# Attention on transposed scores, two heads side by side on the halves of TensorE, in a fused attention and feed-forward kernel

## The chip, the cores and the metric

The kernel runs on one core of a Trainium2 chip. The metric is device time in microseconds, from repeated executions; the trace of one execution gives the span from first to last instruction (1 to 2 us shorter). Engines: PE is TensorE's matmuls, PEld its weight loads, DVE is VectorE, ACT ScalarE, POOL GpSimd, SP the queue that issues most transfers.

## The reference

Attention within hash buckets (a query sees only the keys with the same 6 sign bits), then a feed-forward block with the gate h * erf(softplus(h)).

```python
# q, k, v: (4, 8, 768, 64) fp32; proj: (64, 6)
q_bucket = sum(((q @ proj) > 0) * 2**arange(6));  k_bucket = ...   # per token
scores = where(q_bucket[..., :, None] == k_bucket[..., None, :], q @ k.T / 8, -1e9)
attn = exp(scores - scores.max(-1)); attn = attn / (attn.sum(-1) + 1e-9)
x = (attn @ v) laid out as (3072, 512)
h = x @ w_in                       # (512, 2048)
out = (h * erf(max(h, 0) + log1p(exp(-abs(h))))) @ w_out    # (2048, 512)
```

## The kernel before

One head at a time, 128 queries at a time. The bucket is matched inside the score product: 64 rows of q, then 64 rows of a one-hot bucket, against k and -2^100 where the bucket differs. So each score matmul contracts 128 rows. The softmax runs along the free axis, which needs a maximum, and the result must be transposed before it can weigh v.

```python
def attend(i, c):                       # head i, chunk c of 128 queries
    for half in range(2):
        nc.tensor.matmul(out=sc[:, half, 0:HS], lhsT=d["qa"][:, c*P:(c+1)*P],
                         rhs=d["ka"][:, half*HS:(half+1)*HS], start=True, stop=True)
    nc.vector.reduce_max(out=m, in_=sc[:, :, 0:HS], axis=AX.XY)
    ...                                  # nm = -scale * m
    nc.scalar.activation(out=e, in_=sc, func=AF.Exp, bias=nm, scale=scale, accum_out=z)
    ...                                  # r = 1 / (z + 1e-9);  e = e * r
def turn(i, c, e):                       # six 128x128 transposes, two evictions on ACT
    ...
def weigh(i, half):
    for kc in range(NC):                 # output in 64 partitions: 64 columns of the array
        nc.tensor.matmul(out=av[rows, :], lhsT=d["vt"][:, kc, :], rhs=d["eT"][:, kc, :], ...)
    nc.vector.tensor_copy(out=xT[b][rows, h // 2, ...], in_=av[rows, :])
```

Meanwhile the fp64 weights are loaded and rounded to fp32. The feed-forward stage follows: per period 64 matmuls of the hidden layer and 16 of the output layer, with ACT and DVE computing the gate beside them. The change hardly touches it.

## Time and profile before

| | us |
|---|---|
| time, median of 4 | 1456.19 (1453.61 to 1458.48) |
| attention with its start | 785 |
| feed-forward | 671 |
| TensorE busy, of the span | 97% |

A line of a group reads: source line, engine, operation, output<-inputs, shapes, count | busy time, mean ns of one | idle time of the engine just before, and what ended it. Each fp32 matmul shows as two records. A matmul's mean ns is its latency; what it costs is the spacing of records in the chain of waits, whose lines read start, length, what, count. The prediction below shows the lines of before.

### The profile page before, as it was taken

How to read it: one execution, taken by the hardware profiler on the slowest of the kernel's cores; microseconds unless marked ns; L12 is line 12 of the kernel's file. 1: busy time of each engine (PE TensorE's matmuls, PEld its weight loads, DVE VectorE, ACT ScalarE, POOL GpSimd, SP SyncE). 2: the span in 40 equal slices, each digit the busy share in tenths (PEclk: the TensorE clock that was granted, in tenths of full speed). 3: DMA queues.
4: the chain of work that ended last, by engine and by line, in shares of the span. 5: the costliest groups of instructions: out<-in, count | busy, mean ns of one | idle time of the engine just before them, and what ended most of it. 6: DMA issues, size and time to landing. Idle time of an engine off the chain costs nothing.

```text
span 1455.9 us, 14558 instructions
## 1 busy us (share of the span) xinstructions
PE 1418.3 (97%) x5248; PEld 803.2 (55%) x5248; DVE 1058.9 (73%) x1868; ACT 799.2 (55%) x1201; POOL 144.5 (10%) x102
## 2 busy tenths in 40 slices
PE   7999999999999999999999999999999999999998
PEld 3444444444444444544446866666666666666653
DVE  6888888879887666667662896686686686686684
ACT  2344444444444444445443886676676676676683
POOL 3432143324320000000000000000000000000000
PEclk9999999999999999999999999999999999999999
DMA  5221222212211011111000000000000000000000
GB/s 161 73 70 61 77 75 59 75 60 82 71 53 36 31 44 28 38 28 39 6 1 1 0 0 15 15 1 15 15 1 15 15 0 15 15 0 15 15 1 29
DMA packets 40703, 49.17 MB, mean 34 GB/s; under 512 B 27308, under 2 KB 27320, under 8 KB 40632
## 3 DMA queue, kind: packets, MB, share of 16 engines
q1 hardware_dynamic: 35856, 31.47, 7.2%
q0 software_dynamic: 4608, 16.78, 3.6%
q8 instruction: 41, 0.67, 0.2%
q14 instruction: 30, 0.25, 0.1%
q10 hardware_dynamic: 168, 0.01, 0.0%
HBM read 41.96 MB, written 6.29 MB: 33 GB/s over the span
## 4 chain that ended last, share of the span: by engine, by line
PE 79%; DVE 14%; ACT 2%; issue 2%; POOL 1%; DMA 1%; SPq 0%; ACTq 0%; POOLq 0%; DVEq 0%
PE o_ps L477 21%; PE h_ps L399 21%; PE av L334 14%; PE sc L276 12%; PE tr_ps L319 7%; DVE m L284 3%; PE bits_ps L227 2%; DVE e L304 2%; ACT e L291 1%; DVE qa L254 1%; PE bucket_ps L246 1%; DVE top L197 1%; DVE keep L170 1%; DVE ka L262 1%; DMA qa<-in_qkT_dram 1%
## 5 line engine op out<-in xcount | busy, mean ns | idle before, releaser
L326 ACT COPY eT<-tr_ps 128x384 f32<-128x384 f32 x384 | 171.2, 481 | 321.0 <-PE tr_ps L319 319.7
L477 PE MATMUL o_ps<-w_out_sb,h 128*128 128x512 f32 x768 | 338.5, 595 | 3.6 <-DVE h L466 3.6
L399 PE MATMUL h_ps<-xT,w_in_sb 128*128 128x256 f32 x1536 | 338.5, 379 | 0.0
L399 PEld LDWEIGHTS h_ps<-xT,w_in_sb 128*128 128x128 f32 x1536 | 291.8, 190 | 57.7 <-issue 13.0
L276 PE MATMUL sc<-ka,qa 128*128 128x384 f32 x768 | 299.3, 498 | 11.8 <-ACT e L291 11.1
L334 PE MATMUL av<-eT,vt 128*64 128x384 f32 x768 | 262.8, 492 | 0.0
L477 PEld LDWEIGHTS o_ps<-w_out_sb,h 128*128 128x128 f32 x768 | 146.3, 191 | 171.1 <-issue 162.6
L284 DVE TENSOR_REDUCE m<-sc 128x1 f32<-128x768 f32 x192 | 183.3, 954 | 64.1 <-PE sc L276 61.0
L291 ACT ACTIVATE e<-sc,nm 128x768 f32<-128x768 f32 x192 | 174.1, 907 | 89.9 <-DVE nm L286 87.4
L319 PEld LDWEIGHTS tr_ps<-ident,e 128*128 128x128 f32 x1152 | 127.0, 141 | 120.9 <-issue 49.5
L334 PEld LDWEIGHTS av<-eT,vt 128*64 128x64 f32 x768 | 100.4, 137 | 154.7 <-issue 146.6
L319 PE MATMUL tr_ps<-ident,e 128*128 128x128 f32 x1152 | 177.8, 282 | 7.8 <-DVE e L304 3.5
L276 PEld LDWEIGHTS sc<-ka,qa 128*128 128x128 f32 x768 | 126.4, 192 | 69.6 <-ACT e L291 25.9
L412 ACT COPY h<-h_ps 128x1024 f32<-128x1024 f32 x48 | 48.5, 1011 | 171.3 <-PE h_ps L399 171.3
L458 DVE SCALAR_TENSOR_TENSOR s<-q,s 128x1024 f32<-128x1024 f32 x96 | 111.1, 1220 | 23.0 <-ACT q L457 23.0
L304 DVE TENSOR_SCALAR e<-e,r 128x768 f32<-128x768 f32 x192 | 124.3, 647 | 2.8
L341 DVE COPY xT<-av 64x384 f32<-64x384 f32 x64 | 35.3, 551 | 94.4 <-PE av L334 94.3
L457 ACT ACTIVATE q<-z,cq 128x1024 f32<-128x1024 f32 x96 | 102.1, 1134 | 0.0
L486 DVE COPY ob<-o_ps 128x512 f32<-128x512 f32 x24 | 16.5, 690 | 109.3 <-PE o_ps L477 109.3
L173 POOL TENSOR_SCALAR keep<-keep 128x512 int32<-128x512 int32 x32 | 73.2, 2287 | 92.8 <-DVE nm L286 56.8
L466 DVE TENSOR_TENSOR h<-h,s 128x1024 f32<-128x1024 f32 x48 | 56.6, 1221 | 16.7 <-ACT s L465 16.7
L413 DVE TENSOR_SCALAR e<-h 128x1024 int32<-128x1024 int32 x48 | 33.1, 690 | 45.0 <-ACT h L412 45.0
(43 smaller groups left out, 1100.5 us busy)
## 6 DMA issues: line engine op xcount, KB each, us to landing
qa<-in_qkT_dram SPq DMA_DIRECT2D x32, 384.0 KB, 3.4
raw<-in_w_in_dram POOLq DMA_DIRECT2D x16, 512.0 KB, 4.2
raw<-in_w_out_dram POOLq DMA_DIRECT2D x16, 512.0 KB, 3.8
ka<-in_qkT_dram SPq DMA_DIRECT2D x32, 192.0 KB, 3.7
vt<-in_v_dram SPq DMA_DIRECT2D x32, 192.0 KB, 2.6
out_dram<-ob SPq DMA_DIRECT2D x24, 256.0 KB, 2.0
powers_f<-in_powers_dram ACTq DMA_DIRECT2D x1, 6.0 KB
proj_sb<-in_proj_dram SPq DMA_DIRECT2D x1, 6.0 KB, 1.7
```

Of the source, the lines that this page charges most:

```text
L173: nc.gpsimd.tensor_scalar(out=keep, in0=keep, scalar1=float((1023 - 126) << 20), scalar2=-1.0, op0=ALU.is_ge, op1=ALU.mult,)
L276: nc.tensor.matmul(out=sc[:, half, 0:HS], lhsT=d["qa"][:, c * P : (c + 1) * P], rhs=d["ka"][:, half * HS : (half + 1) * HS], start=True, s ...
L284: nc.vector.reduce_max(out=m, in_=sc[:, :, 0:HS], axis=AX.XY)
L291: nc.scalar.activation(out=e[:, :].rearrange("p (h k) -> p h k", h=2), in_=sc[:, :, 0:HS], func=AF.Exp, bias=nm[:, 0:1], scale=scale, accu ...
L304: nc.vector.tensor_scalar(out=e, in0=e, scalar1=r[:, 0:1], scalar2=None, op0=ALU.mult)
L319: nc.tensor.transpose(out=ps[:, j * P : (j + 1) * P], in_=e[:, kc * P : (kc + 1) * P], identity=ident,)
L326: nc.scalar.copy(out=dst, in_=src)
L334: nc.tensor.matmul(out=av[rows, :], lhsT=d["vt"][:, kc, :], rhs=d["eT"][:, kc, :], start=(kc == 0), stop=(kc == NC - 1),)
L399: nc.tensor.matmul(out=ps[:, f, :], lhsT=w_in_sb[:, kc, (g * G + f) * P : (g * G + f + 1) * P], rhs=xT[b][:, kc, t0 : t0 + T], start=(kc = ...
L457: nc.scalar.activation(out=q, in_=z, func=AF.Square, bias=cq[:, j : j + 1])
L458: nc.vector.scalar_tensor_tensor(out=s, in0=q, scalar=r, in1=s, op0=ALU.add, op1=ALU.mult)
L477: nc.tensor.matmul(out=ps, lhsT=st[t * NG + f // G]["h"][:, f % G, tt * P : (tt + 1) * P], rhs=w_out_sb[:, f, :], start=(f == 0), stop=(f ...
```

## The change

Scores are computed transposed (keys on partitions), so exp's output can weigh v without any transpose. Heads go in pairs: the scores of head A contract rows 0-63 of the array and those of head B rows 64-127; the weighted sums of A leave through columns 0-63 and those of B through columns 64-127. The bucket mask becomes a bf16 matmul of sign bits that is accumulated ahead of the fp32 scores. No maximum is subtracted: exp is safe while a bound on |scores|, checked on the chip during the feed-forward stage, is at most 40. If not, a branch at the end repeats everything by a general path (not taken with these inputs). Sums over keys, now along partitions, are added up on VectorE and finished by a matmul with ones; the divisors go through DRAM to be inverted compactly and broadcast. A query with no matching key gets the mean of v: half of the weighted sums have a 385th column, of ones, for it, and its scaled result is `ev` below.

```diff
-        def attend(i, c):      # score, max, exp with bias and sum, scale
-        def turn(i, c, e):     # transposes and evictions
+            def scores(n):
+                d["st"] = [big("st") for _ in range(GC)]
+                for part, src in enumerate(("b", "")):        # bf16 bits, then fp32
+                    for c in range(GC):
+                        for ab in range(2):
+                            rows = slice(ab * D, ab * D + D)
+                            nc.tensor.matmul(out=d["st"][c][:, ab, 0:HS],
+                                lhsT=d["k" + src][rows, keys], rhs=d["q" + src][rows, cols], ...)
+            def sum_keys(n):   # d["sum"] += e, on VectorE, 128x768 a time
+            def weigh(n):
+                for c in range(GC):
+                    for ab in range(2):
+                        rows = slice(ab * D, ab * D + D)
+                        nc.tensor.matmul(out=d["av"][rows, 0:w],
+                            lhsT=d["v"][:, g * GC + c, rows], rhs=e[:, ab, 0:w], ...)
+            def divisor(n):    # ones x sum, both heads
 ...
+            for n in range(NS + 4):          # 16 pairs x 4 steps
+                scores(n); taking = bits(i + 1, r)
+                sum_keys(n - 1); weigh(n - 1)
+                exponentials(n); taking()
+                if (n - 1) % 2 == 1: divisor(n - 1); leave(n - 1)
+                if r == 0 and i >= 1: spread(i - 1)      # z to DRAM and back, compact
+                if r == 2 and i >= 1: invert(i - 1)      # 1/z to DRAM, broadcast back as r
+                if r == 3 and i >= 1: normalise(i - 1)   # x = (x + ev) * r, on VectorE
 ...
+            def extremes(m):   # feed-forward: reload q and k, absolute maxima on VectorE
+    def judge():               # bound of all heads: a load, a product, flag
+    again = nc.values_load(flag[0:1, 0:1], min_val=0, max_val=1)
+    with tc.If(again > 0):
+        general()
+        feed_forward(None)
```

## The prediction

> **What bounds the kernel now.** I read the page first (who is busy), then the groups by form (what the busy engine does), then the two stages as windows, then the chain of waits inside one head.
>
> From the page: the totals, the utilisation row of TensorE, and the chain that ended last.
>
> ```profile
> PE 1418.3 (97%) x5248; PEld 803.2 (55%) x5248; DVE 1058.9 (73%) x1868; ACT 799.2 (55%) x1201; POOL 144.5 (10%) x102
> ...
> PE   7999999999999999999999999999999999999998
> ...
> PE 79%; DVE 14%; ACT 2%; issue 2%; POOL 1%; DMA 1%; SPq 0%; ACTq 0%; POOLq 0%; DVEq 0%
> ```
>
> TensorE is busy 97% from the second slice on, and is 79% of the chain. The kernel is bound by TensorE in both stages, so a change is worth what it takes out of TensorE's stream, as long as no other engine comes up behind it.
>
> The two stages, from the windows view (attention, then feed-forward; the first scores start at 14.15 us and the last weighted sum ends at 784.8 us):
>
> ```profile
> 14.00:785.00 771.00, 749.36 (x2936) 364.27 (x2936) 585.33 (x1399) 350.98 (x769) 139.96 (x92) 1.00 0.17 50
> 785.00:1456.00 671.00, 663.31 (x2304) 437.83 (x2303) 468.32 (x457) 448.19 (x432) 0.00 (x0) 1.00 0.03 10
> ```
>
> Columns are window, length, then busy time and count of PE, PEld, DVE, ACT, POOL. Attention takes 785 us with its start and feed-forward 671 us; TensorE fills both (97% and 99%).
>
> The groups of the attention stage on TensorE, and the work on ACT and DVE that the change touches:
>
> ```profile
> L276 PE MATMUL sc<-ka,qa 128*128 128x384 f32 x768 | 299.3, 498 | 11.8 <-ACT e L291 11.1
> L334 PE MATMUL av<-eT,vt 128*64 128x384 f32 x768 | 262.8, 492 | 0.0
> L284 DVE TENSOR_REDUCE m<-sc 128x1 f32<-128x768 f32 x192 | 183.3, 954 | 64.1 <-PE sc L276 61.0
> L291 ACT ACTIVATE e<-sc,nm 128x768 f32<-128x768 f32 x192 | 174.1, 907 | 89.9 <-DVE nm L286 87.4
> L326 ACT COPY eT<-tr_ps 128x384 f32<-128x384 f32 x384 | 171.2, 481 | 321.0 <-PE tr_ps L319 319.7
> L304 DVE TENSOR_SCALAR e<-e,r 128x768 f32<-128x768 f32 x192 | 124.3, 647 | 2.8
> L319 PE MATMUL tr_ps<-ident,e 128*128 128x128 f32 x1152 | 177.8, 282 | 7.8 <-DVE e L304 3.5
> ```
>
> Scores 299, weighted sums 263, transposes 178; with bits 51.5 and buckets 34.5 (two smaller rows of the same view) that is the 750 us above, give or take overlap. The 492 ns mean of one record is its latency; the cost is the spacing. The chain of waits gives it (start, length, what, records):
>
> ```profile
> 704.21 4.01 PE av L334 x12
> 708.22 0.80 PE tr_ps L319 x6
> 709.03 1.29 PE sc L276 x4
> 710.32 0.66 PE tr_ps L319 x6
> ```
>
> Scores: 1.29/4 = **0.322 us a record** of 384 columns. Each fp32 matmul is two records (192 score chunks x 2 halves = 384 matmuls, 768 records), so 0.644 us. Twelve av records should take 12 x 0.322 = 3.86 and take 4.01; six transposes right after av take 0.80, elsewhere 0.66. So going into and out of the 64-column form costs about **0.15 us** each time.
>
> **What the Trainium skill says.**
> 1. "TensorE: Matmul & The Clock Gate", section "Part 3: Packing small matmuls — row/col tiling": matmuls with other row or column groups run concurrently, starts some 4 ns apart, and still issue in order; 4 row tiles gave 3.07x, 3 column tiles 2.38x. The trace before has no two groups side by side, so it neither agrees nor disagrees.
> 2. "TensorEngine Tiling (Array Packing)", section "Key Properties": a change of the tiling mode drains the engine. The trace agrees, with the 0.15 us above.
> 3. "FP8 and Floating Point Precision", section "TensorE Precision Notes": true fp32 is four passes. [...]So a bf16 matmul of 384 columns is half a record, an estimate of 0.16 us.
> 4. "VectorE: DVE Perf Modes", section on the TRN2 errata: an fp32 tensor_tensor takes (N+151)/0.96 ns. For 1024 that is 1224; the trace has 1221 to 1225. For 768 it gives 957 ns.
>
> **The change, part by part.** A step of the new loop is 384 queries x 3 key chunks x 2 heads; 16 pairs x 4 = 64 steps.
>
> *Removed from TensorE:* all transposes (178 us) and the bucket matmuls (34 us). *Moved onto half arrays:* scores now contract 64 rows and the two heads of a pair lie in rows 0-63 and 64-127; the weighted sums of the two heads lie in columns 0-63 and 64-127. The mask becomes an extra bf16 matmul per score tile. *Added:* divisor matmuls. Bits stay: 64 fp32 matmuls.
>
> The instruction order is head A, head B, A, B, with both records of A ahead of B's. If issue is in order, A's second record waits for A's first, then B's first starts beside A's second: overlap two deep, one record late. N records in one mode then take (N/2+1) x 0.322. TensorE per step:
> - hash part: 6 bf16 matmuls, 3 x 0.16 = 0.5.
> - fp32 scores: 12 records, 7 x 0.322 = 2.25.
> - bits of the next pair: 2 x 0.322 = 0.64 (absent in the last 4 steps).
> - weighted sum: 12 records, 2.25; in every other step with 4 divisor records, 9 x 0.322 = 2.90; mean 2.58.
> - three mode switches, 3 x 0.15 = 0.45.
>
> Sum 6.42; x 64 = 411; less 3 for the missing bits, plus 3 for the last weighted sum: **411 us**.
>
> Beside it, ACT: a 384-column eviction takes 481 ns and a 1024-column one 1011, so 0.83 ns a column plus 163; 768 columns without the accumulator read about 800. 192 exps = 154, 32 signs of q = 15, 64 evictions = 31, 64 weight operations of 512 at 0.59 = 38: 238 us, 58% of 411. All eT copies (171) go. DVE: 160 sums of 768 at 0.957 = 153; weight rounding 568+697+695+412+677 ns = 3.05 a piece, x 32 = 98; bits of k 32 x 0.62 = 20; normalising 16 x 0.96 = 15: 286 us, 70%. Both fit under TensorE. The score buffers: step n+1 needs the three PSUM tiles that ACT empties in step n; ACT ends them about 1.5 us after the last score, while TensorE has bits and weighted sum (over 3 us) to do. No new wait if the overlap is as assumed. The divisors' round trips through DRAM have two to three steps, 13 us or more, of slack.
>
> *Start:* first scores at 14 us before. Now four bit matmuls pass one PSUM bank one by one: 17 us. *Feed-forward:* 48 halves of 6.9 us each for both products are unchanged: 671. New there: 64 loads and 64 absolute maxima of 384 columns (0.55 us by the 954 ns row), 35 us of DVE, in a stage where DVE is 70% busy; two buffers, so DVE also waits for loads. Off the path; I allow 6 us. *End:* flag read and branch on each engine, 4 us. The general path is not run.
>
> Sum: 17 + 411 + 671 + 6 + 4 = 1109. I add 2% of the attention (8) for waits that a tight loop always has, and 1.3 as runs are longer than the span: about **1118 us**, 0.77 of before.
>
> **The rivals.**
> - *The halves do not overlap* (fp32 in two records, in-order issue). Per step: 0.96 + 3.86 + 0.64 + 14 x 0.322 + 0.45 = 10.4, x 64 = 667. Time 17 + 667 + 681 + 9 = about 1370. For it: nothing in the trace shows overlap, and the skill's runs are not said to be fp32. Against: weight loads are already hidden behind the matmul before (137 ns in 322).
> - *Only one kind overlaps.* Rows not: 2.07 more a step, 132 us, about 1250. Columns not (two fp32 streams through all 128 rows): 1.93 more, 124 us, about 1240.
> - *DVE or ACT becomes the bound.* DVE at 286 of 411 would have to be slowed 40%, or waits on the round trips must block it. It would give 1150 to 1200. ACT would need more still.
> - *The check in feed-forward delays gates*: DVE from 70% to over 80% with load waits; up to 30 us, 1150.
> - *Better than assumed*: no lag of one record, 0.322 less twice a step: 1080.
>
> **Range and chances.** Full overlap 65%, one kind only 20%, none 13%, something unforeseen 2%. Even without overlap the removed transposes and buckets leave it 6% faster. So 1118, range 1070 to 1245 (it takes in the one-kind rivals, and leaves out no overlap). Faster 0.95, within 2% 0.03, slower 0.02.
>
> **What the changed profile would show.** Right: attention's last matmul near 430 us, steps of 6.4 to 6.6 us with TensorE still 95% busy, score tiles of two heads finishing within one record of each other, twelve weighted-sum records in about 2.3 us; ACT near 240 and DVE near 290 in attention; feed-forward within 10 us of 671; ACT waiting for TensorE and not the reverse. Wrong: scores or weighted sums 0.322 apart a record (no overlap); TensorE idle ahead of scores because of exponentials, or ahead of divisors because of the DVE sums; switches much above 0.15 us; feed-forward halves above 6.9 us.

## The result, and the profile after

| | before | after |
|---|---|---|
| time, median | 1456.19 us | 1128.34 us (1125.14 to 1134.24, 4 runs) |
| ratio | | 0.7754, 95% interval 0.7719 to 0.7788 |
| first scores start | 14 us | 18 us |
| attention after that | 771 us | 423 us |
| feed-forward to the last instruction | 671 us | 685 us |

A ratio is the mean time of one kernel's fast runs over that of the other's of the same rounds, so not quite the ratio of the medians quoted. The predicted 1118 us with 1070 to 1245 held. From the page of after, the same rows as shown of before, with the granted clock by slice added:

```profile
PE 1057.3 (94%) x4482; PEld 608.6 (54%) x4482; DVE 809.8 (72%) x962; ACT 678.0 (60%) x785; POOL 77.9 (7%) x68
...
PE   5999898999989987989999999999999998999987
...
PEclk9999999999999998999999999999999998999999
...
PE 75%; DVE 12%; DMA 8%; issue 2%; ACT 1%; SPq 1%; DVEq 0%
```

TensorE is still the bound, but in the attention slices (the first sixteen) it is no longer full, and the chain now runs for 8% through transfers, where before it was 1%. The groups by form say who is waiting:

```profile
L308 PE MATMUL st<-q,k 64*128 64x384 f32 x768 | 140.8, 501 | 0.0
...
L344 PE MATMUL av<-e,v 128*64 128x385 f32 x384 | 69.2, 495 | 0.0
L344 PE MATMUL av<-e,v 128*64 128x384 f32 x384 | 68.8, 494 | 0.0
...
L308 PE MATMUL st<-qb,kb 64*128 64x384 bf16 x384 | 45.7, 347 | 0.0
...
L356 PE MATMUL z_ps<-sum,ones 128*64 128x384 f32 x128 | 29.9, 545 | 36.8 <-DVE sum L332 36.8
...
L417 DVE SCALAR_TENSOR_TENSOR xT<-xT,ev,r 128x768 f32<-128x768 f32 x16 | 16.3, 1019 | 41.4 <-DMA r<-rd 41.4
```

Scores and weighted sums have as many fp32 records as before (768 each), but 141 and 138 us of busy time in place of 299 and 263. The transposes are gone. The last two lines are a pair: VectorE stands 41.4 us before normalising, for the broadcast of r, and TensorE stands 36.8 us before the divisors, for VectorE's sums. In the chain of waits of one pair of heads:

```profile
205.84 0.97 DVE sum L332
206.80 0.14 issue
206.94 1.55 PE z_ps L356 x4
208.49 3.45 PE st L308 x18
211.94 0.84 PE bits L191 x2
212.78 2.09 PE av L344 x12
214.87 2.53 PE st L308 x18
217.40 0.84 PE bits L191 x2
218.25 2.12 PE av L344 x12
```

An undisturbed step is the last three lines, 2.53 + 0.84 + 2.12 = 5.49 us. After the late divisor the same 18 score records take 3.45 us: over the 1.55 us of the divisor records the granted clock was 0.50, and over the 3.45 us it was 0.73, after TensorE had stood for 2.13 us. Why the sums are late shows in VectorE's own order of work, from the timeline of after (start, length, instruction, idle time before):

```profile
193.90 0.23 DVE L401 RECIPROCAL zc<-zc 128x12 f32<-128x12 f32 x1
...
197.11 0.68 DVE L199 TENSOR_SCALAR kb<-bits,kcol_sb 128x384 bf16<-128x384 f32 x1
200.12 1.02 DVE L417 SCALAR_TENSOR_TENSOR xT<-xT,ev,r 128x768 f32<-128x768 f32 x1 [2.33 <-DMA r<-rd]
...
202.84 3.95 DVE L332 TENSOR_TENSOR sum<-sum,e 128x768 f32<-128x768 f32 x3
```

The inverse is ready at 194.1. It is written out and read back broadcast, which lands at 200.1. VectorE reaches the normalising at 197.8 and waits; behind it, in order, stand three instructions of the weight rounding and then the three sums that TensorE's divisor needs.

### The profile page after: what moved, and what is told of

The parts are those of the page before. It is cut to its first block, busy times and chain, and to the rows that moved or that the text cites. A ratio compares the mean times of both kernels' runs of the same rounds, so it can differ in the third digit from the quotient of the medians.

```text
span 1126.5 us, 11846 instructions
## 1 busy us (share of the span) xinstructions
PE 1057.3 (94%) x4482; PEld 608.6 (54%) x4482; DVE 809.8 (72%) x962; ACT 678.0 (60%) x785; POOL 77.9 (7%) x68
## 4 chain that ended last, share of the span: by engine, by line
PE 75%; DVE 12%; DMA 8%; issue 2%; ACT 1%; SPq 1%; DVEq 0%
PE h_ps L567 28%; PE o_ps L645 28%; PE st L308 9%; PE av L344 6%; DMA r<-rd 5%; DVE sum L332 5%; PE bits L191 3%; DMA rd<-zc 2%; PE z_ps L356 2%; DVE xT L417 1%; DVE rest L285 1%; DVE top L274 1%; ACT xT L370 1%; SPq L408 1%; DVE unit L282 1%
## 5 line engine op out<-in xcount | busy, mean ns | idle before, releaser
L645 PE MATMUL o_ps<-w_out_sb,h 128*128 128x512 f32 x768 | 338.5, 595 | 7.5 <-DVE h L634 7.5
L567 PE MATMUL h_ps<-xT,w_in_sb 128*128 128x256 f32 x1536 | 342.6, 382 | 0.0
L320 ACT ACTIVATE e<-st 128x768 f32<-128x768 f32 x192 | 141.9, 809 | 92.0 <-PE st L308 89.2
L332 DVE TENSOR_TENSOR sum<-sum,e 128x768 f32<-128x768 f32 x128 | 150.7, 1177 | 9.3 <-DVE sum L332 0.5
L308 PE MATMUL st<-q,k 64*128 64x384 f32 x768 | 140.8, 501 | 0.0
L344 PE MATMUL av<-e,v 128*64 128x385 f32 (+1 forms) x768 | 137.9, 495 | 0.0
L308 PEld LDWEIGHTS st<-q,k 64*128 64x128 f32 x768 | 75.6, 198 | 41.6 <-issue 6.6
L344 PEld LDWEIGHTS av<-e,v 128*64 128x64 f32 x768 | 49.5, 136 | 80.6 <-issue 71.7
L654 DVE COPY ob<-o_ps 128x512 f32<-128x512 f32 x24 | 16.4, 687 | 79.8 <-PE o_ps L645 79.8
L356 PE MATMUL z_ps<-sum,ones 128*64 128x384 f32 x128 | 29.9, 545 | 36.8 <-DVE sum L332 36.8
L598 DVE TENSOR_TENSOR w<-e,w 128x1024 f32<-128x1024 f32 x48 | 58.8, 1225 | 1.7
L608 DVE SCALAR_TENSOR_TENSOR s<-s,w 128x1024 f32<-128x1024 f32 x48 | 58.8, 1225 | 1.6
L605 DVE SCALAR_TENSOR_TENSOR s<-h,s 128x1024 f32<-128x1024 f32 x48 | 58.5, 1219 | 0.0
L626 DVE SCALAR_TENSOR_TENSOR s<-z,s 128x1024 f32<-128x1024 f32 x48 | 56.5, 1220 | 0.0
```

The costliest lines, as they stand in the source:

```text
L308: nc.tensor.matmul(out=d["st"][c][:, ab, 0:HS], lhsT=d["k" + src][rows, keys], rhs=d["q" + src][rows, cols], start=(part == 0), stop=(part ...
L320: nc.scalar.activation(out=e[:, :, 0:HS], in_=st[:, :, 0:HS], func=AF.Exp, scale=scale)
L332: nc.vector.tensor_tensor(out=d["sum"], in0=d["sum"], in1=e, op=ALU.add)
L344: nc.tensor.matmul(out=d["av"][rows, 0:w], lhsT=d["v"][:, g * GC + c, rows], rhs=e[:, ab, 0:w], start=(g == 0 and c == 0), stop=(g == 1 an ...
L567: nc.tensor.matmul(out=ps[:, f, :], lhsT=w_in_sb[:, kc, (g * G + f) * P : (g * G + f + 1) * P], rhs=xT[b][:, kc, t0 : t0 + T], start=(kc = ...
L598: nc.vector.tensor_tensor(out=w, in0=e, in1=w, op=ALU.subtract)
```

## The experiments

Eight runs, each timed in three rounds. The first four share one chip and one set of runs of before (1455.25 us), the last four another (1456.84 us).

### Are the halves really side by side, and in what order do they start?

**Scores grouped by head.** The same matmuls, A A A B B B in each part; correct.

```diff
-                    for c in range(GC):
-                        for ab in range(2):
+                    for ab in range(2):
+                        for c in range(GC):
```

> Score matmuls of a step issued head by head (A,A,A,B,B,B) in place of A,B,A,B; same arithmetic, correct result. Theory 'halves overlap and starts are in program order': the overlap is lost except at the seams, a step's 18 score records go from 2.5 us to about 4.3, 64 steps x 1.8 = 115 us more; the 37 us in which TensorE now waits for DVE sums is covered by the longer steps, so 1205 to 1245 us. Rival 'each half has its own queue and runs ahead of program order': 2.5 us a step, 1125 to 1135. Rival 'there is no overlap, the after kernel is fast for other reasons': no change either, but then 18 records could not have fitted in 2.5 us.

Measured 1145.38 us (ratio 0.7874, 0.7861 to 0.7887): neither theory. **Weighted sums grouped by head**, the same exchange of loops in `weigh`:

> Weighted-sum matmuls of a step issued head by head. Theory as for the scores: 12 records go from 2.1 us to about 3.7 (11 x 0.322 and the switch), 64 x 1.6 = 103 us more, less up to 37 us of covered wait: 1195 to 1232. Rival 'own queues': 1125 to 1135.

Measured 1142.75 us (0.7854, 0.7841 to 0.7867): neither again. In the chains of waits, first of the scores run, then of the sums run, 18 score records take 3.28 us (2.53 in after) and 12 weighted-sum records 2.79 us (2.09):

```profile
219.85 3.28 PE st L308 x18
```

```profile
214.36 2.79 PE av L344 x12
```

The order matters, but far less than strict order would have it (4.3 and 3.7). Take off the 0.15 us of the mode switch: 2.64 us is 8.2 records of 0.322. Head A has six. So B starts when A still has about four of its six to go. The sums run also shows directly that starts leave program order; this is its timeline of TensorE:

```profile
222.44 0.49 PE L356 MATMUL z_ps<-sum,ones 128*64 128x384 f32 x1
222.50 0.49 PE L344 MATMUL av<-e,v 128*64 128x385 f32 x1
```

The divisor of head A (columns 0-63) stands behind all of B's weighted sums in the program, and starts before the last of them. The totals rose by only 17 and 14 us where 64 steps of 0.75 and 0.70 us more would be 48 and 45: the longer steps cover part of the wait for the sums, which fell from 36.8 to 16.3 and 18.1 us, and the stretches of half clock that followed some of these waits in after (below) are gone: before the last wait these two runs have none.

So I formed another theory, that one half may start while about four records of the other are still ahead of it, and tested it together with a control, both built on the repaired kernel (x3_late_norm, below) so that no wait covers anything. **Nine records of A, then nine of B** (head as the outermost loop of `scores`; correct):

> On x3_late_norm: a step's nine score records of head A (3 bf16, 6 fp32), then the nine of head B. Grouping by head within each part gave 3.28 us for 18 records where strict order would give 4.3 and free queues 2.5. Theory 'the other half may start while about four records of the first are still ahead of it': B starts when A has four left, at 2.41 - 1.29 = 1.12, and ends at 3.53 + 0.15 = 3.7 us; 64 x 1.15 = 74 us over x3_late_norm: 1145 to 1165. Rival 'free queues, the 3.28 came from something else': 2.5 to 2.9 us, below 1110. Rival 'strict order': 4.7 us, above 1210.

Measured 1148.67 us (0.7888, 0.7875 to 0.7902), as expected. The timeline of TensorE shows B's first bf16 records 1.15 us after A's, expected 1.12, with three of A's fp32 records begun; the chain of waits gives 3.68 us for the step's scores, expected 3.7:

```profile
211.39 0.66 PE L308 MATMUL st<-qb,kb 64*128 64x384 bf16 x3
211.88 1.13 PE L308 MATMUL st<-q,k 64*128 64x384 f32 x3
212.54 0.49 PE L308 MATMUL st<-qb,kb 64*128 64x384 bf16 x2
```

**Control: both heads on one half** (wrong result, relative error 0.99, since head B reads head A's rows):

```diff
-                            rows = slice(ab * D, ab * D + D)
+                            rows = slice(0, D)
                             nc.tensor.matmul(out=d["st"][c][:, ab, 0:HS], ...
```

> Control, wrong result on purpose, built on x3_late_norm: the scores of both heads read rows 0-63, so all score matmuls of a step are on the same half of the array; counts, sizes and order unchanged. Theory 'the two halves run side by side': without it the 18 records of a step take 6 x 0.16 + 12 x 0.322 + 0.15 = 4.98 us in place of 2.53, 64 x 2.45 = 157 us more than x3_late_norm: 1225 to 1245 us. Rival 'a 64-row matmul is fast by itself, half the rows take half the time': no change, 1078 to 1090.

Measured 1236.84 us (0.8493, 0.8479 to 0.8507), 157 us above x3_again of the same chip, as expected. Chain of waits:

```profile
207.04 4.95 PE st L308 x18
```

4.95 us in place of 2.53. A 64-row matmul is no shorter than a 128-row one; the gain on scores from the halves comes from two of them at once. For the columns no such control was run. There the comparison is with before, where twelve records of the same form took 4.01 us and here 2.09.

### Is the stall VectorE's wait for the broadcast?

**Normalising one step later**, after the sums (correct):

```diff
-                if r == 3 and i >= 1:
-                    normalise(i - 1)
+                if r == 0 and i >= 2:
+                    normalise(i - 2)
 ...                                   # and normalise(NPAIR - 1) after the loop
```

> The normalising of a pair is emitted one step later on VectorE, after the three sums that the divisor needs. Theory 'VectorE stands still for the broadcast of r (41 us) and so the sums and the divisor are late (TensorE idle 37 us)': that wait goes, steps stay at 5.5 us, 1085 to 1097 us. Rival 'VectorE is simply too loaded for 5.5 us steps, or another wait takes its place': TensorE still waits for the sums, 1115 to 1130.

Measured 1081.80 us (0.7443, 0.7414 to 0.7473), better than expected. No added engine time, no smaller amount of work: the same instructions in another order. Its chain of waits over a pair of steps:

```profile
203.35 2.53 PE st L308 x18
205.88 0.88 PE bits L191 x2
206.76 2.08 PE av L344 x12
208.84 0.65 PE z_ps L356 x4
209.49 2.53 PE st L308 x18
```

The divisor takes 0.65 us where it took 1.55, and no score records are slowed. TensorE's wait for the sums is 2.6 us, the last one. Attention lasts 375 us (17.4 to 392.1) in place of 423: 36.8 - 2.6 = 34 us are the wait itself. Of the other 14 or so, 12 are the same TensorE records taking longer in after: scores 140.8 + 45.7 us busy against 135.3 + 42.8, divisors 29.9 against 26.1. The granted clock of after says why, in two stretches of the windows view (TensorE busy is the second number, the granted clock the third from the end):

```profile
203.50:206.92 3.42, 1.31 (x10) 0.30 (x5) 3.21 (x4) 0.48 (x1) 1.94 (x2) 1.00 0.26 43
206.92:210.33 3.41, 3.39 (x14) 1.59 (x16) 2.73 (x4) 1.77 (x3) 0.00 (x0) 0.50 0.34 129
```

The clock was at one half for 3.41 us, then full again. In the attention of after this happened six times before the last wait, from 125.0, 152.3, 179.6, 206.9, 234.2 and 415.1 us. These starts lie whole multiples of 3.41 us apart, so they fit a fixed grid, and in the stretch of the grid before each one TensorE had stood still for 2.1 to 2.7 us. Other stretches before the last wait, with up to 1.88 us of standing (94.28 to 97.69), were followed by full speed. So a wait cost clock only where enough of it fell into one stretch. The limit isn't exact: in before, 1.48 us were once enough (51.4 to 54.8). Six stretches at one half are worth 6 x 3.41 / 2 = 10 us.

VectorE is busy 305 of 374 us in the attention of x3_late_norm, and that is not too much.

It was run again beside the last kernels:

> x3_late_norm again, on the chip of the three kernels above that are built on it, so that they are compared on one chip: 1078 to 1086 us.

1080.19 us (0.7418, 0.74 to 0.7436).

### What does the bound check cost?

**Without check, flag, branch and general path** (right for these inputs only): `feed_forward(None)` in place of `feed_forward(judge)`, the branch removed.

> Bound check, flag, branch and the general path taken out (right for these inputs only). Theory: the check costs TensorE its wait for the judging matmul (3.4 us and a colder clock after it), one load wait at the first gate (2.4 us) and about 2.4 us at the end: 1117 to 1122. Rival 'hidden': 1126 or more.

Measured 1120.01 us (0.7679, 0.764 to 0.7718), so 8 us by the medians, 11 by the ratios, with wide intervals that nearly touch. The traces show where: the feed-forward stage lasts 674.3 us, in after 685.3, as TensorE's wait before the first output product fell from 4.6 to 0.7 us and that for the judging product (3.4) is gone; the attention, which the edit does not touch, was 5 us longer in this execution, with eight stretches at half clock. From the last eviction's end to the last instruction it is 3.3 us, in after 5.7 us: flag and branch cost 2.4 us. The check is cheap, but not hidden.

### A version that beats both

x3_late_norm with the projection loaded on ACT's queue, two banks for the first four bit products, the check's maxima from the fourth period on with four buffers in place of two, and the judging product three periods after its load; correct.

> x3_late_norm and four small repairs: the projection is loaded on the other queue and the first four bit products use two banks (start 3 to 4 us earlier), the bound check's maxima start four periods later with four buffers (no load wait ahead of the first gate, 2.4 us), and the judging product is issued three periods after its load (no 3.4 us wait, no colder clock after it). If each wait is on the path as read: 9 to 12 us less than x3_late_norm, 1066 to 1074. Rival 'they are hidden or come back at another place': 1078 to 1086 as x3_late_norm.

Measured 1068.96 us (0.7342, 0.733 to 0.7354), 11 us less than x3_again on the same chip, as expected in sum but not in each part. TensorE's waits of x3_again, then of x7_best (who waited for what: us in total, times, longest):

```profile
PE bits L191 <- DMA q<-in_qkT_dram: 11.3, 6, 8.8
PE o_ps L646 <- DVE h L635: 7.5, 2, 4.6
PE bound L716 <- DVE mk L714: 3.4, 1, 3.4
```

```profile
PE bits L191 <- DMA v<-in_v_dram: 11.1, 1, 11.1
PE o_ps L650 <- DVE h L639: 7.8, 3, 4.8
```

The judging product's wait is gone. The start did not gain the 3 to 4 us: first scores at 16.4 in place of 17.4 us, as the first bits still wait for transfers until 11.1. The wait for the first gates fell from 4.6 to 0.7 us; of the 7.8 above, 7.1 stand after 1000 us, near the end, where x3_again waits 2.9, so part of the gain came back there, and why is not shown. The first output product starts 49.2 us after the attention's end, in x3_late_norm 54.8. Of the 12.9 us between the two profiled executions 1.1 are the start, 6.9 the feed-forward stage, and 4.9 the attention from its first scores on, at which no repair aimed (1.9 of these are the first step's scores, 2.53 us in place of 4.42). That the sum came out as expected is in part luck.

## Why the prediction was right, point by point

- **TensorE stays the bound, and a step is what it does per step.** Right in kind. The terms: scores with their hash part 2.53, predicted 2.75 plus a switch; weighted sums 2.09, predicted 2.25 plus a switch; bits of the next pair 0.84 against 0.64 plus a switch; divisor 0.65 undisturbed against the 0.65 put in (2.90 - 2.25). A step without disturbance is 2.53 + 0.84 + 2.09 + 0.33 = 5.79, not 6.42. The estimate of 0.16 us for a bf16 record held: in the one-half control six in a row took 0.99 us (206.97 to 207.96).
- **"overlap two deep, one record late": this step failed.** The halves do overlap (the control: 4.95 against 2.53), but there is no lag of one record: twelve records take six slots and a switch. A half can start ahead of records of the other half that come before it in the program, about four of them by the runs by head. That lag, 0.322 us twice a step, is 41 us over 64 steps. The rival "better than assumed" named it, with 1080 us; the kernel with the stall repaired took 1081.80.
- **"The divisors' round trips through DRAM have two to three steps, 13 us or more, of slack": this failed too.** I counted from the divisor to the normalising. The last leg, from the inverse to the broadcast r, has less than one step: 6.0 us of transfers from 194.1 to 200.1, against 3.7 us until VectorE arrives. And I looked only at who needs r, not at what stands behind the normalising in VectorE's order. It cost 48 us of attention (423 against 375), where I had put 8 us for waits. The prediction's own signs of being wrong name it (TensorE idle ahead of divisors because of the DVE sums), and the third rival (VectorE held by the round trips, 1150 to 1200) had the mechanism, but set beside my slower steps.
- **So the sum held by luck, because two errors nearly cancelled**: 411 + 8 predicted for attention, 423 measured; 41 us less for the overlap, 40 us more for the stall.
- **A reading of before was loose.** The five groups named for its 750 us sum to 826: busy times of groups overlap at their ends. By the chain six transposes cost 0.66 to 0.80 us, so all 192 sets 127 to 154 us, not 178. Nothing in the predicted sum rests on it.
- **VectorE and ScalarE beside TensorE**: right. In the attention of x3_late_norm, VectorE was busy 305 us (predicted 286) and ScalarE 226 (238).
- **Start 17, feed-forward and end 681**: 18 and 685. The feed-forward halves are 6.9 us as before; what was added are the wait for the first gates (4.6 us, before 0.7), the judging product (3.4), the end (2.4), and 4 us of longer hidden-layer records (342.6 against 338.5), with stretches at half clock from 435.6, 497.0 and 937.4 us. The other 2.9 us of the 7.5 that TensorE waits for gates stand near the end, as in before.
- **No overlap at all, or rows alone not overlapping** would have cost 157 us on scores by the control (predicted 132 over my lagged sum). These rivals are ruled out for scores by a run, for the sums by comparison with before only. Of the 396 us by which the attention of the repaired kernel is shorter than that of before (375 against 771), the halves are 157 on the scores by the control and an estimated 123 on the sums (64 x (4.01 - 2.09)). The remaining 116 are what went (transposes, bucket products) less what came in; no run splits them.

What stays open: whether the limit of about four records is a count of records or of instructions including weight loads, and what sets the limit of standing time beyond which the clock falls. Of the 48 us of the stall, 34 are wait and 10 to 12 clock by the traces; no run holds the clock to test it.

## What to carry to other kernels

Where a matmul fills only half of the array's rows or columns, put two independent ones on the two halves, and alternate them in the program: the same work took half the time here. After such a gain, look down each in-order engine for an instruction that waits for a round trip, and ask what stands behind it: moving one VectorE instruction past the sums was worth some 46 us, and short waits of TensorE can cost again through the clock. When a prediction lands, check its terms one by one; this one was right with two wrong terms.

## What the Trainium skill lacked or had wrong

- "TensorE: Matmul & The Clock Gate", section "Part 3: Packing small matmuls — row/col tiling", says matmuls start and end strictly in program order. The runs show starts out of order between halves (222.44 ahead of 222.50 above), and a reach of about four records: 12 records grouped by head took 2.79 us, where strict order would need 3.7. Ends are modelled in these traces, so nothing is shown on ends.
- The same page, section "Part 1: The HAM clock gate (the "warmup" mystery)", puts the fall of the clock at an idle window of about 3.4 us. The stretches at half clock are that long here (3.41 us), but the one before needn't be idle throughout: 2.11 us of standing in it (203.50 to 206.92) were followed by a clock of 0.50, 1.88 us (94.28 to 97.69) were not. The page tells of shorter idles that lower the clock too, but not how short.
- "TensorEngine Tiling (Array Packing)", section "Key Properties", tells that a mode change drains the engine, not what it costs: about 0.15 us here, before and after (4.01 - 3.86 and 2.09 - 1.93).
- No page says whether fp32 matmuls overlap on halves. They do: 18 records of scores, 12 of them fp32, 2.53 us against 4.95 on one half, 12 of weighted sums 2.09 us against 4.01 alone.
- "Runtime: NRT & Kernel Launch", section "Instruction fetch mechanics", warns of branches, and it and "Advanced Engine Details and Errata", section "Control Flow Timing", have figures for a single register load and a single branch, but no page has one for a whole flag read and a branch past the general path at a program's end: 2.4 us here (5.7 against 3.3 without).
